# The last batch's side work in another order: smaller steps of the leftover choice, low parts of weights between VectorE and GpSimd

## The chip, the cores and the metric

One Trainium2 chip, one core. The metric is the device time of one execution in microseconds (us). The engines are TensorE (PE; PEld is its weight loading), VectorE (DVE), ScalarE (ACT), GpSimd (POOL) and SyncE (SP), whose queue issues most of the transfers.

## The reference

Attention over pooled keys and values (8 batches, 8 heads, 576 positions, head width 64), whose output, 4608 tokens of 512 numbers, goes through a mixture of 16 experts in 4 groups. Each token takes its best group and in it its best expert.

```python
scores = scale * np.matmul(q, k_p.transpose(0, 1, 3, 2))
...
g_idx = np.argmax(x @ w_group, axis=1)
...
e_idx = np.argmax(xg @ w_expert[g], axis=1)
...
h = np.maximum(xg[mask_e] @ w1[g, e], 0.0)
ye = h @ w2[g, e]
out[tok_idx] = combined[:, None] * ye
```

## The kernel before

**Batches and plans.** The work goes batch by batch. Strings of pieces (`START`, `FIRST`, `SECOND`, `STEADY`, `LAST`) write down by hand in which order the pieces are issued; each engine does its own instructions in just this order, and waits at each for what it needs. `LAST` is the plan of the last batch, in which there is no attention of a next batch to fill in.

**The main expert of a batch.** Almost all tokens of a batch choose one expert. Its weights are fetched and the whole batch goes through them. Every weight block is held as two fp32r parts: `m.cast:m:j` (ScalarE, line 579) makes the high part of quarter j of matrix m, `m.lo:m:j` (line 585) makes the low part by a subtraction, on GpSimd unless the piece ends in `:v` (VectorE). `m.up:f:h` is the first product for hidden block f and token half h: 12 matmuls (line 602) and a relu on ScalarE (line 604). `m.upd:f:h` makes the low part of the hidden values on VectorE (line 610 for the first half, the three instructions of line 615 for the second) and frees the accumulator. There are three of these (pool `ps_m`), so the fourth product after one waits for that one's `upd`. `m.down:z` is a piece of the second product, 8 matmuls (lines 631 and 642; 663 for the last 128 rows).

**Leftover tokens.** Tokens of other experts are collected in blocks of 32. `Left.place` counts and ranks them in steps, one for each `l.step` of the plan (lines 733 to 771, most on VectorE). `l.which` (lines 778 to 785, VectorE) then chooses the block's batch and expert, and SyncE loads the two numbers into registers (lines 786 to 788). Only then can `l.fetch_x` (line 834) fetch the two parts of that batch's x from memory into `pT` and `xr`, cleared by `l.xtiles` (line 824, GpSimd); `l.fetch_a` and `l.fetch_b` fetch the expert's weights behind it. `l.whole:c` (line 848) adds the two parts of x, for odd c on GpSimd, for even c on VectorE. `l.rows` (line 816) and `l.turn:c` (line 858) are TensorE pieces that stand in the plan between the last up products and the down products; `l.turn:3`, the first turn, reads what `l.whole:3` wrote. The rest of the block's products (lines 866 to 896) stands between later down pieces.

Of the kernel before, what the change touches and what calls it, by code (L numbers as in the profile page):

```python
# [30 lines left out]
BS = 32  # L31
# [34 lines left out]
x.su_:0 x.nm:0:p w.lo:1:1 m.down:10 m.down:11 m.down:12 w.cast:1:2 m.down:13 w.cast:1:3  # L66
"""
LAST = """
m.load:2:3 m.load:2:2 m.up:0:0 p.tail m.upd:0:0 m.lo:1:2:v m.up:0:1 l.step m.upd:0:1 m.up:1:0 l.step l.step m.upd:1:0 m.up:1:1 l.step l.step m.upd:1:1 l.xtiles
m.up:2:0 m.cast:2:1 l.step m.upd:2:0 l.step m.up:2:1 l.step m.upd:2:1 l.step m.up:3:0 l.step l.step m.upd:3:0 m.up:3:1 l.step l.step m.upd:3:1  # L70
m.up:5:0 l.step l.step l.step l.step m.upd:5:0 m.lo:1:3 m.cast:2:2 m.up:4:0 l.step l.step l.which m.lo:2:2:v m.upd:4:0 m.lo:2:1:v
m.up:6:0 m.cast:2:0 m.upd:6:0 m.up:5:1 m.lo:2:0:v m.up:4:1 m.up:6:1 m.cast:2:3 l.fetch_x l.tiles m.upd:5:1 m.upd:4:1 m.upd:6:1 l.slots m.down:0 m.down:1 l.fetch_a:1
m.up:7:0 l.fetch_b:1 m.upd:7:0 l.whole:4 l.whole:0 m.up:7:1 l.rows l.next_ l.whole:3 m.upd:7:1 l.turn:3 l.turn:4 m.down:12
l.whole:1 l.turn:1 l.turn:0 l.whole:2 m.lo:2:3:p m.down:2 m.down:3 l.turn:2 m.down:4 l.gather m.down:5 l.back m.down:6 l.up m.down:7 l.hback
m.down:8 l.down l.fetch_x l.fetch_a l.fetch_b m.down:13 m.down:9 m.down:10 l.slots m.down:11
# [4 lines left out]
def attn_moe(ctx: ExitStack, tc: tile.TileContext, q, k, v, wg, we, w1, w2, out):  # L80
    nc = tc.nc
# [603 lines left out]
    class Left:  # L685
# [22 lines left out]
        def place(s):  # L708

            kb = wk.tile([128, NC, 2, D], F32, name="kb").rearrange("p g x d -> p g (x d)")  # L710
            s.lt_, s.colf, tri = kb[:, 0], kb[:, 1], kb[:, 2]
            kp = wk.tile([128, 6, D], F32R, name="v6", bufs=2).rearrange("p g d -> p (g d)")
            onesr, trir = kp[:, 0:128], kp[:, 128:256]

            nc.gpsimd.affine_select(out=tri, in_=ones, pattern=[[1, 128]], compare_op=ALU.is_gt, fill=0.0, base=0, channel_multiplier=-1)
            nc.scalar.copy(out=trir, in_=tri)
            nc.scalar.copy(out=onesr, in_=ones)
            yield

            nc.gpsimd.iota(s.colf, [[0, 4], [1, BS]], base=0, channel_multiplier=0, allow_small_or_imprecise_dtypes=True)  # L720
            sl = sq.tile([128, NC * DM], F32, name="q")
            s.sl = [sl[:, 128 * c:128 * c + 128] for c in range(NC)]
            s.xg, s.xs, s.h = sl[:, 640:768], sl[:, 768:896], sl[:, 896:1152]
            s.hT = sl[:, 1152:1408].rearrange("p (t x) -> p t x", t=2)
            s.y = sl[:, 1408:1536]
            s.tmp = wk.tile([128, H * SP], F32, name="kT")
            kv = sk.tile([128, 5, 512], F32, name="kv").rearrange("p a x -> p (a x)")
            tot, rank = [kv[:, o:o + 640].rearrange("p (b c e) -> p b c e", b=B, c=NC) for o in (0, 640)]
            lf = loh.rearrange("p b c e -> p (b c e)")
            for lhs, dst in ((onesr, tot), (trir, rank)):  # L730
                for o, n in ((0, 320), (320, 320)):
                    ps = ps_t.tile([128, 512], F32, name="tp")
                    nc.tensor.matmul(ps[:, 0:n], lhsT=lhs, rhs=lf[:, o:o + n], start=True, stop=True)
                    nc.vector.tensor_copy(out=dst.rearrange("p b c e -> p (b c e)")[:, o:o + n], in_=ps[:, 0:n])
                    yield
            for c in range(1, NC):

                tt(out=rank[:, :, c, :], in0=rank[:, :, c, :], in1=tot[:, :, c - 1, :], op=ALU.add)
                tt(out=tot[:, :, c, :], in0=tot[:, :, c, :], in1=tot[:, :, c - 1, :], op=ALU.add)
                yield  # L740

            sc_ = sk.tile([128, 5, 512], F32, name="vv").rearrange("p a x -> p (a x)")
            nb, exc = sc_[:, 0:128], sc_[:, 128:256].rearrange("p (b e) -> p b e", e=NE)
            nbi = sc_[:, 256:384].bitcast(I32)
            ts(out=nb.rearrange("p (b e) -> p b e", e=NE), in0=tot[:, :, NC - 1, :], scalar1=float(BS - 1), scalar2=None, op0=ALU.add)
            nc.vector.tensor_copy(out=nbi, in_=nb)
            yield
            ts(out=nbi, in0=nbi, scalar1=5, scalar2=None, op0=ALU.logical_shift_right)
            nc.vector.tensor_copy(out=nb, in_=nbi)
            yield  # L750
            nc.vector.tensor_tensor_scan(out=s.cum, data0=ones, data1=nb, initial=0.0, op0=ALU.mult, op1=ALU.add)
            tt(out=exc.rearrange("p b e -> p (b e)"), in0=s.cum, in1=nb, op=ALU.subtract)
            yield

            for c in range(NC):
                stt(out=rank[:, :, c, :], in0=exc, scalar=float(BS), in1=rank[:, :, c, :], op0=ALU.mult, op1=ALU.add)
                yield
            stt(out=rank, in0=rank, scalar=1.0 + 2.0 ** 20, in1=loh.bitcast(F32), op0=ALU.add, op1=ALU.mult)
            red(out=s.pos, in_=rank, axis=AX.X, op=ALU.add)
            ts(out=s.pos, in0=s.pos, scalar1=-1.0 - 2.0 ** 20, scalar2=None, op0=ALU.add)  # L760
            yield

            for c, (o, n) in enumerate(CH):
                nc.gpsimd.iota(s.meta[:, c, :, 0], [[4 * S, B]], base=4 * (o - int(BIG)), channel_multiplier=4, allow_small_or_imprecise_dtypes=True)
                if c < 4:
                    nc.gpsimd.iota(s.meta[:, c, 0:1, 0], [[0, 1]], base=4 * (256 * (c // 2) + c % 2 - int(BIG)), channel_multiplier=8, allow_small_or_imprecise_dtypes=True)
            nc.gpsimd.tensor_copy(out=s.meta[:, :, :, 1], in_=gate.rearrange("p b c -> p c b"))
            nc.vector.memset(s.it, 0.0)

            ts(out=s.tmp[:, 0:1], in0=s.cum[:, B * NE - 1:B * NE], scalar1=-1.0, scalar2=0.0, op0=ALU.add, op1=ALU.max)  # L770
            nc.vector.tensor_copy(out=s.niti, in_=s.tmp[:, 0:1])
            yield
# [228 lines left out]
```

## Time and profile before

| what | us |
|---|---|
| median of 3 runs | 514.22 (513.57 to 514.29) |
| the profiled execution's own time | 514.15 |
| its span, first to last instruction | 512.4 |
| TensorE busy in it | 501.1 (98%) |
| VectorE busy | 345.6 (67%) |
| GpSimd busy | 281.6 (55%) |

Times in the profile count from the start of the span; the 1.75 us between the span and the execution's time lie outside it. A busy TensorE says only that matmuls are in flight. The mean granted TensorE clock is 0.993 of full speed. The last batch's up products begin at 447.77 us.

### The profile page before, as it was taken

The numbers are of one execution on the slowest core, as the hardware profiler recorded it, in microseconds if no ns is written. First come the engines' busy times: TensorE is split into PE (matmuls) and PEld (weight loads), VectorE is DVE, ScalarE is ACT, GpSimd is POOL, SyncE is SP. The second block draws the span as 40 slices with busy tenths as digits, with TensorE's granted clock in tenths as the row PEclk, the third lists the DMA queues.
The fourth block names the chain that finished last, engine by engine and source line by source line (L and its number), as shares of the span: only waits on it lengthen the run. The fifth ranks groups of instructions, "written<-read, shape, count | busy, mean of one in ns | idle before, by whom it ended". The sixth has DMA issues, their size and how long they took to land.

```text
span 512.4 us, 14902 instructions
## 1 busy us (share of the span) xinstructions
PE 501.1 (98%) x6085; PEld 440.1 (86%) x6085; DVE 345.6 (67%) x928; ACT 206.3 (40%) x385; POOL 281.6 (55%) x246
## 2 busy tenths in 40 slices
PE   8899999999999999999999999999999999998996
PEld 6688987998889978899789988899789988898976
DVE  6876877899385869486784768476784764199702
ACT  2354432545216542455216551455325551344212
POOL 2386666576518595476828585476947471830400
PEclk9799999999999999999999999999999999999999
DMA  8699299685428966954197615985055100923751
GB/s 279 191 260 205 24 280 236 124 192 137 77 92 242 265 106 176 318 150 80 29 308 213 151 26 138 368 311 89 1 191 192 43 3 22 304 96 114 271 172 58
DMA packets 118110, 83.70 MB, mean 163 GB/s; under 512 B 71034, under 2 KB 93818, under 8 KB 117784
## 3 DMA queue, kind: packets, MB, share of 16 engines
q1 hardware_dynamic: 113408, 75.67, 54.7%
q10 hardware_dynamic: 4600, 7.02, 4.0%
q8 instruction: 49, 0.80, 0.7%
q14 instruction: 21, 0.17, 0.1%
q0 software_dynamic: 32, 0.04, 0.0%
HBM read 77.28 MB, written 28.53 MB: 206 GB/s over the span
## 4 chain that ended last, share of the span: by engine, by line
PE 76%; DVE 10%; DMA 5%; ACT 2%; POOL 2%; issue 2%; SPq 1%; ACTq 0%; DVEq 0%; POOLq 0%
PE mm L602 30%; PE mm L631 27%; PE mm L642 4%; PE sc L396 4%; PE sc L336 4%; DMA vv<-in_v_dram 2%; DMA sw<-in_moe_w_dram 2%; PE tp L429 1%; PE mm L663 1%; POOL w L585 1%; DVE s L368 1%; DVE ht L615 1%; DVE pT L382 1%; PE tp L425 1%; DVE p L357 1%
## 5 line engine op out<-in xcount | busy, mean ns | idle before, releaser
L631 PE MATMUL mm<-w,ht 128*128 128x512 f32 x744 | 172.6, 385 | 0.0
L585 POOL TENSOR_TENSOR w<-sw,w 128x1024 fp32r<-128x1024 f32 (+2 forms) x86 | 145.2, 1711 | 33.7 <-ACT w L579 29.2
L631 PEld LDWEIGHTS mm<-w,ht 128*128 128x128 f32 x744 | 136.8, 189 | 25.2 <-issue 6.4
L602 PE MATMUL mm<-xb,w 128*128 128x288 f32 (+1 forms) x768 | 109.6, 294 | 1.7 <-DVE ht L610 1.7
L602 PEld LDWEIGHTS mm<-xb,w 128*128 128x128 f32 x768 | 100.7, 189 | 6.1 <-ACT w L579 2.2
L602 PE MATMUL mm<-xa,w 128*128 128x288 f32 (+1 forms) x768 | 100.2, 283 | 0.5 <-ACT xa L401 0.5
L602 PEld LDWEIGHTS mm<-xa,w 128*128 128x128 f32 x768 | 95.5, 190 | 2.2 <-ACT xa L401 0.9
L604 ACT ACTIVATE ht<-mm 128x288 fp32r<-128x288 f32 (+2 forms) x128 | 51.9, 410 | 87.1 <-PE mm L602 85.4
L375 POOL TENSOR_TENSOR p<-p,su 128x864 f32<-128x864 f32 (+2 forms) x30 | 40.3, 1343 | 78.6 <-DVE su L370 67.7
L579 ACT CAST w<-sw 128x1024 fp32r<-128x1024 f32 x64 | 66.7, 1042 | 31.5 <-DMA sw<-in_moe_w_dram 29.0
L615 DVE SCALAR_TENSOR_TENSOR ht<-mm,ht 128x64 fp32r<-128x64 f32 (+4 forms) x192 | 37.7, 252 | 25.8 <-ACT ht L604 25.5
L636 ACT ACTIVATE y<-mm,gm 128x512 f32<-128x512 f32 x31 | 21.2, 684 | 66.4 <-PE mm L631 66.4
L362 ACT ACTIVATE p<-p 128x864 f32<-128x864 f32 (+2 forms) x30 | 23.4, 780 | 37.5 <-DVE p L357 29.6
L368 DVE TENSOR_REDUCE s<-p 128x12 f32<-128x864 f32 (+2 forms) x30 | 25.8, 861 | 15.1 <-ACT p L362 15.1
L382 DVE STREAM_TRANSPOSE pT<-p 128x960 f32<-128x960 f32 (+2 forms) x30 | 29.2, 972 | 8.0 <-POOL p L375 7.2
L610 DVE SCALAR_TENSOR_TENSOR ht<-mm,ht 128x288 fp32r<-128x288 f32 (+1 forms) x64 | 26.9, 422 | 10.4 <-ACT ht L604 10.4
L642 PE MATMUL mm<-w,ht 128*128 128x512 f32 x128 | 29.5, 381 | 0.0
L336 PEld LDWEIGHTS sc<-kT,qT 64*32 64x32 f32 x2176 | 23.7, 105 | 6.3 <-issue 3.5
L336 PE MATMUL sc<-kT,qT 64*32 64x72 f32 x2176 | 28.5, 229 | 0.5 <-DVE qT L322 0.2
L675 DVE TENSOR_TENSOR y<-mm,y 64x512 f32<-64x512 f32 x8 | 5.5, 682 | 33.6 <-ACT y L647 20.2
L396 PE MATMUL sc<-pT,v 32*64 32x288 f32 (+2 forms) x384 | 26.9, 409 | 0.2 <-DVE p L357 0.2
L396 PE MATMUL tp<-pT,v 32*64 32x288 f32 (+2 forms) x384 | 26.9, 409 | 0.0
(227 smaller groups left out, 568.8 us busy)
## 6 DMA issues: line engine op xcount, KB each, us to landing
sw<-in_moe_w_dram SPq DMA_DIRECT2D x72, 512.0 KB
vv<-in_v_dram SPq DMA_DIRECT2D x27, 320.0 KB
q<-in_q_dram SPq DMA_DIRECT2D x112, 72.0 KB
kv<-in_k_dram SPq DMA_DIRECT2D x14, 512.0 KB
out_dram<-y ACTq DMA_DIRECT2D x23, 256.0 KB
xscr<-xa SPq DMA_DIRECT2D x5, 1152.0 KB
xscr<-xb SPq DMA_DIRECT2D x5, 1152.0 KB
xscr<-xb SPq DMA_DIRECT2D x3, 1280.0 KB
```

The source lines that it names most:

```text
L336: nc.tensor.matmul(ps[x][32 * g:32 * g + 32, SP * t:SP * t + SP], lhsT=s.qT[c][64 * x:64 * x + 64, g, 32 * t:32 * t + 32], rhs=s.kT[64 * x ...
L368: red(out=two[:, :, :, 0], in_=p.rearrange("p t (x s) -> p t x s", x=2), axis=AX.X, op=ALU.add)
L375: (nc.vector if eng == "v" else nc.gpsimd).tensor_tensor(out=p, in0=p, in1=bc(s.su[c][:, 0:w], SP), op=ALU.mult)
L382: nc.vector.transpose(out=s.pT[:, :, o:o + n].rearrange("p j (t i) -> p t j i", i=32), in_=probs[:, z:z + n // 32].rearrange("p t (j i) -> ...
L396: nc.tensor.matmul(banks[a][64 * x:64 * x + 64, 0:n], lhsT=s.v6[32 * a:32 * a + 32, 5 if x and i == 0 else j, :], rhs=s.pT[32 * a:32 * a + ...
L579: nc.scalar.copy(out=s.w[m, j][0], in_=raw)
L585: (nc.vector if eng == "v" else nc.gpsimd).tensor_tensor(out=wl[:, i:i + n], in0=s.raw[m, j][:, i:i + n], in1=wh[:, i:i + n].bitcast(F32), ...
L602: nc.tensor.matmul(ps[:, 0:n], lhsT=l[:, kc, fs], rhs=apart(s.a.xt[hf][:, r, kc]), start=(kc == 0 and i == 0), stop=(kc == 3 and i == 2))
L604: nc.scalar.activation(out=halves(ht[:, sl]), in_=joined(ps[:, 0:n]), func=AF.Relu)
L615: stt(out=ht[:, at:at + hi - lo], in0=ps[:, a, lo:hi], scalar=0.0, in1=ht[:, t + lo:t + hi].bitcast(F32), op0=ALU.max, op1=ALU.subtract)
L631: nc.tensor.matmul(ps, lhsT=s.ht[f][:, 640 * l + o:640 * l + o + 128], rhs=apart(s.w[2, f // 2][r][:, f % 2, :]), start=(i == 0), stop=(i ...
L642: nc.tensor.matmul(ps, lhsT=s.ht[f][:, 512:640], rhs=apart(s.w[2, f // 2][r][:, f % 2, :]), start=(i == 0), stop=(i == 15))
```

## The change

Two things change, both of them for the last batch. In `Left.place` the first step is cut in two: the triangle mask and the column numbers (GpSimd) come first, the two fp32r casts (ScalarE) in a step of their own. And `LAST` is written anew in its first lines: the first step stands ahead of everything, the other steps are shared out differently among the up products, the low parts 1:2, 1:3 and 2:0 go to GpSimd ahead of the clearing of `pT` and `xr`, and 2:1 and 2:2 stay on VectorE, the first right behind `m.upd:2:0`, the second right behind `m.upd:5:1`. The order of the up products is the same. From `MANUAL` on, every line number is one lower.

```diff
 LAST = """
-m.load:2:3 m.load:2:2 m.up:0:0 p.tail m.upd:0:0 m.lo:1:2:v m.up:0:1 l.step m.upd:0:1 m.up:1:0 l.step l.step m.upd:1:0 m.up:1:1 l.step l.step m.upd:1:1 l.xtiles
-m.up:2:0 m.cast:2:1 l.step m.upd:2:0 l.step m.up:2:1 l.step m.upd:2:1 l.step m.up:3:0 l.step l.step m.upd:3:0 m.up:3:1 l.step l.step m.upd:3:1
-m.up:5:0 l.step l.step l.step l.step m.upd:5:0 m.lo:1:3 m.cast:2:2 m.up:4:0 l.step l.step l.which m.lo:2:2:v m.upd:4:0 m.lo:2:1:v
-m.up:6:0 m.cast:2:0 m.upd:6:0 m.up:5:1 m.lo:2:0:v m.up:4:1 m.up:6:1 m.cast:2:3 l.fetch_x l.tiles m.upd:5:1 m.upd:4:1 m.upd:6:1 l.slots m.down:0 m.down:1 l.fetch_a:1
+l.step m.load:2:3 m.load:2:2 m.lo:1:2 m.lo:1:3 m.up:0:0 p.tail m.upd:0:0 m.up:0:1 l.step m.cast:2:0 m.upd:0:1 m.lo:2:0 m.up:1:0 l.step l.step m.upd:1:0 m.up:1:1 l.step l.step m.upd:1:1 l.xtiles
+m.up:2:0 m.cast:2:1 l.step m.upd:2:0 m.lo:2:1:v m.up:2:1 l.step m.upd:2:1 m.up:3:0 l.step l.step m.upd:3:0 m.up:3:1 l.step l.step m.cast:2:2 m.upd:3:1
+m.up:5:0 l.step l.step m.upd:5:0 m.up:4:0 l.step l.step l.step l.step m.upd:4:0 m.up:6:0 l.step m.upd:6:0 m.up:5:1 l.step l.which m.upd:5:1 m.up:4:1 m.lo:2:2:v m.upd:4:1 m.up:6:1 m.cast:2:3 l.fetch_x l.tiles m.upd:6:1 l.slots m.down:0 m.down:1 l.fetch_a:1
 m.up:7:0 l.fetch_b:1 m.upd:7:0 l.whole:4 l.whole:0 m.up:7:1 l.rows l.next_ l.whole:3 m.upd:7:1 l.turn:3 l.turn:4 m.down:12
...
             nc.gpsimd.affine_select(out=tri, in_=ones, pattern=[[1, 128]], compare_op=ALU.is_gt, fill=0.0, base=0, channel_multiplier=-1)
+            nc.gpsimd.iota(s.colf, [[0, 4], [1, BS]], base=0, channel_multiplier=0, allow_small_or_imprecise_dtypes=True)
+            yield
             nc.scalar.copy(out=trir, in_=tri)
             nc.scalar.copy(out=onesr, in_=ones)
             yield
-
-            nc.gpsimd.iota(s.colf, [[0, 4], [1, BS]], base=0, channel_multiplier=0, allow_small_or_imprecise_dtypes=True)
```

On VectorE before, from the `upd` of the up product 2:0 (line 610) on, only steps of the ranking follow until the `upd` of 2:1 (line 615):

```order
L610 SCALAR_TENSOR_TENSOR ht<-mm,ht 128x288
L738 TENSOR_TENSOR kv<-kv 128x8x16
L739 TENSOR_TENSOR kv<-kv 128x8x16
L738 TENSOR_TENSOR kv<-kv 128x8x16
L739 TENSOR_TENSOR kv<-kv 128x8x16
L615 SCALAR_TENSOR_TENSOR ht<-mm,ht 128x144
```

The same place in the changed kernel:

```order
L609 SCALAR_TENSOR_TENSOR ht<-mm,ht 128x288
L584 TENSOR_TENSOR w<-sw,w 128x1024
L737 TENSOR_TENSOR kv<-kv 128x8x16
L738 TENSOR_TENSOR kv<-kv 128x8x16
L614 SCALAR_TENSOR_TENSOR ht<-mm,ht 128x144
```

The low part 2:1 (line 585, now 584) has come in here, and one step has moved behind the `upd` of 2:1.

On VectorE before, this stands between the last ranks and the first instruction of `l.which` (line 778), with the `upd` of 5:0 as the only one of line 610:

```order
L756 SCALAR_TENSOR_TENSOR kv<-vv,kv 128x8x16 x4
L610 SCALAR_TENSOR_TENSOR ht<-mm,ht 128x288
L758 SCALAR_TENSOR_TENSOR kv<-kv,loh 128x640
L759 TENSOR_REDUCE pos<-kv 128x40
L760 TENSOR_SCALAR pos<-pos 128x40
L768 MEMSET it 128x1
L770 TENSOR_SCALAR kT<-cum 128x1
L771 CAST niti<-kT 128x1
L778 TENSOR_SCALAR kb<-cum,it 128x128
```

The same place in the changed kernel, with the `upd`s of 5:0, 4:0 and 6:0:

```order
L609 SCALAR_TENSOR_TENSOR ht<-mm,ht 128x288
L755 SCALAR_TENSOR_TENSOR kv<-vv,kv 128x8x16 x4
L609 SCALAR_TENSOR_TENSOR ht<-mm,ht 128x288
L757 SCALAR_TENSOR_TENSOR kv<-kv,loh 128x640
L758 TENSOR_REDUCE pos<-kv 128x40
L759 TENSOR_SCALAR pos<-pos 128x40
L609 SCALAR_TENSOR_TENSOR ht<-mm,ht 128x288
L767 MEMSET it 128x1
L769 TENSOR_SCALAR kT<-cum 128x1
L770 CAST niti<-kT 128x1
L777 TENSOR_SCALAR kb<-cum,it 128x128
```

The `upd`s of 4:0 and 6:0, which stood behind `l.which`, now stand ahead of it.

On GpSimd before, in the last batch (line 585 twice for 1:0 and 1:1, then the mask, the column numbers, the two clearings, 1:3, and the first number of `meta`):

```order
L585 TENSOR_TENSOR w<-sw,w 128x1024 x2
L715 AFFINE_SELECT kb<-ones 128x128
L720 IOTA kb 128x128
L824 MEMSET pT 128x2304
L824 MEMSET xr 128x2304
L585 TENSOR_TENSOR w<-sw,w 128x1024
L764 IOTA meta 128x8
```

The same place in the changed kernel:

```order
L584 TENSOR_TENSOR w<-sw,w 128x1024 x2
L714 AFFINE_SELECT kb<-ones 128x128
L715 IOTA kb 128x128
L584 TENSOR_TENSOR w<-sw,w 128x1024 x3
L823 MEMSET pT 128x2304
L823 MEMSET xr 128x2304
L763 IOTA meta 128x8
```

Three low parts (1:2, 1:3, 2:0) now stand ahead of the clearings, where one stood behind them. The orders of TensorE and of SyncE are the same in both kernels.

## Rows read from the trace of the kernel before

**Rows 1.** The page's busy lines and the shares of the chain that ended last.

```profile
PE 501.1 (98%) x6085; PEld 440.1 (86%) x6085; DVE 345.6 (67%) x928; ACT 206.3 (40%) x385; POOL 281.6 (55%) x246
...
PE 76%; DVE 10%; DMA 5%; ACT 2%; POOL 2%; issue 2%; SPq 1%; ACTq 0%; DVEq 0%; POOLq 0%
```

**Rows 2.** Waits, 444 to 513 us: who waited for whom, us, times, longest.

```profile
POOL pT L848 <- DMA xr<-xscr: 23.8, 1, 23.8
...
PE mm L602 <- DVE ht L610: 1.7, 1, 1.7
```

**Rows 3.** TensorE's timeline: start, us, line, tiles, count, [idle before <-releaser].

```profile
464.53 1.63 PE L602 MATMUL mm<-xb,w 128*128 128x288 f32 x12
467.84 3.24 PE L602 MATMUL mm<-xb,w 128*128 128x288 f32 x24 [1.68 <-DVE ht L610]
...
477.53 1.26 PE L816 MATMUL tp<-kT,q 128*128 128x2 f32 x10
478.79 1.09 PE L858 MATMUL tp<-ident,pT 128*128 128x128 f32 x8
...
502.61 5.52 PE L663 MATMUL mm<-w,ht 128*128 128x256 f32 x48
```

**Rows 4.** VectorE's timeline in the last batch.

```profile
450.34 2.69 DVE L585 TENSOR_TENSOR w<-sw,w 128x1024 fp32r<-128x1024 f32 x1
...
456.35 0.46 DVE L610 SCALAR_TENSOR_TENSOR ht<-mm,ht 128x288 fp32r<-128x288 f32 x1
456.72 0.28 DVE L738 TENSOR_TENSOR kv<-kv 128x128 f32<-128x128 f32 x1
...
464.50 0.19 DVE L760 TENSOR_SCALAR pos<-pos 128x40 f32<-128x40 f32 x1
...
466.14 0.14 DVE L785 TENSOR_SCALAR ki<-ki 128x1 int32<-128x1 int32 x1
466.20 1.22 DVE L585 TENSOR_TENSOR w<-sw,w 128x1024 fp32r<-128x1024 f32 x1
467.33 0.45 DVE L610 SCALAR_TENSOR_TENSOR ht<-mm,ht 128x288 fp32r<-128x288 f32 x1
467.70 1.22 DVE L585 TENSOR_TENSOR w<-sw,w 128x1024 fp32r<-128x1024 f32 x1
```

**Rows 5.** ScalarE's timeline: casts of weights (1:2, 1:3 and 2:1).

```profile
445.69 1.05 ACT L579 CAST w<-sw 128x1024 fp32r<-128x1024 f32 x1 [0.49 <-ACT y L636]
...
448.45 1.04 ACT L579 CAST w<-sw 128x1024 fp32r<-128x1024 f32 x1
...
456.21 1.04 ACT L579 CAST w<-sw 128x1024 fp32r<-128x1024 f32 x1
```

**Rows 6.** SyncE's timeline: the issue of the first fetch of x.

```profile
468.66 0.36 SPq L834 DMA_DIRECT2D pT<-xscr  x1
```

**Rows 7.** GpSimd's timeline: a clearing, a low part, and `l.whole:3` alone.

```profile
444.69 2.01 POOL L824 MEMSET pT<- 128x2304 f32 x1
...
449.58 2.36 POOL L585 TENSOR_TENSOR w<-sw,w 128x1024 fp32r<-128x1024 f32 x1 [0.92 <-ACT w L579]
...
477.23 1.50 POOL L848 TENSOR_TENSOR pT<-pT,xr 128x512 f32<-128x512 f32 x1 [23.83 <-DMA xr<-xscr]
```

**Rows 8.** VectorE's timeline at the program's start.

```profile
2.68 1.11 DVE L113 TENSOR_SCALAR hm<-flath 128x40 f32<-128x40 f32 x1
```

**Rows 9.** GpSimd's timeline at the program's start.

```profile
2.57 1.18 POOL L117 MEMSET p<- 128x1280 f32 x1
```

**Rows 10.** Stretches: us; busy PE, PEld, DVE, ACT, POOL; granted clock; DMA share, GB/s.

```profile
16.00:20.00 4.00, 3.16 (x37) 2.65 (x36) 3.34 (x14) 0.99 (x3) 0.10 (x1) 0.72 0.23 45
20.00:24.00 4.00, 3.38 (x72) 2.80 (x73) 3.19 (x7) 2.37 (x5) 2.79 (x5) 0.50 1.00 323
24.00:28.00 4.00, 3.52 (x57) 2.29 (x55) 1.25 (x4) 2.06 (x5) 4.00 (x6) 0.93 1.09 297
...
466.00:470.00 4.00, 2.32 (x19) 2.16 (x18) 3.97 (x8) 0.87 (x3) 0.00 (x0) 1.00 0.19 32
```

## Prediction

> **What bounds the kernel now.** I read the page's busy lines and chain first: TensorE is busy 98% of the span and holds 76% of the chain [rows 1]. So a change of order can win only where TensorE stands idle, and lose wherever it makes TensorE wait. The waits of the last batch come next: TensorE waits once there, 1.7 us, for an instruction of line 610 on VectorE [rows 2]. TensorE's timeline shows where: 5:1 begins at 464.53, then TensorE is idle 1.68 us, and 4:1 begins at 467.84 [rows 3]. It waits for the accumulator of 4:0, freed by the `upd` at 467.33, which stands on VectorE behind the whole choice of the leftover block (done with line 785 at 466.28) and behind a low part of 1.13 us, the distance from 466.20 to 467.33 [rows 4]. This stall is the one thing to be won here: 1.68 us, 0.33%.
>
> There is a second place, and no wait is listed for it, since it only just holds. `l.turn:3` starts on TensorE at 478.79, right after the ten small products of `l.rows` [rows 3]. It needs `l.whole:3`, which GpSimd runs from 477.23 for 1.50 us, to 478.73, after waiting for the transfer of x [rows 7, 2]. Result and reader are 0.06 us apart: TensorE would have arrived at 477.11 without its stall, and would then have waited here for the same 1.68 us. So the stall at 466 costs nothing by itself; **the chain that decides is choice on VectorE, registers on SyncE, transfer of x, `l.whole:3`, first turn**. Its lengths: line 785 ends at 466.28, the first fetch issues at 468.66, 2.38 us later [rows 4, 6]; the sum of both parts begins at 477.23, 8.57 us after the issue; its first use is 1.56 us after that. From the first turn to the last matmul's end, 508.13, TensorE's timeline has no idle time [rows 3]. So the end moves one for one with the end of `l.whole:3`, whatever happens ahead of it, unless TensorE itself is later.
>
> **The change, part by part.**
>
> *The choice on VectorE.* VectorE meets the `upd` of 2:0 at 456.35 in both orders, since that waits for its relu; what VectorE saves before this (the low part 1:2, 2.69 us) only turns into waiting. From 456.35 to 466.28 it is full. The new order puts three more instructions into this stretch and takes none out: the low part 2:1, and the `upd`s of 4:0 and 6:0. The low part takes 1.13 us (the 2.69 of the first one lay beside a low part on GpSimd, below), an `upd` of line 610 takes 0.37 (467.33 to 467.70) [rows 4]. Before the low part can start, its cast must end: ScalarE casts 2:1 from 456.21 to 457.25, behind the relu of 2:0 as before [rows 5], and VectorE, free at 456.72, waits 0.53 us. Sum: 0.53 + 1.13 + 0.37 + 0.37 = **2.40 us later**, so the choice ends at 468.7 where it ended at 466.3. Fewer gaps between dependent steps may give back 0.2.
>
> *The fetch.* SyncE's order is the same, with the same loads behind the fetch, so I keep 2.38 and 8.57 us: issue at 471.1, x there at 479.6, `l.whole:3` done at 481.1. The clearings on GpSimd, which the fetch must follow, end by about 459.2 in the new order (three low parts of 2.36 us, the last from about 452.9, then two clearings of 2.0 [rows 7]), 12 us before it: covered.
>
> *The stall at 466.* It goes. The `upd` of 4:0 comes ahead of line 758. That of 6:0 follows line 760, which ended at 464.69 and now ends 0.53 + 1.13 + 0.37 = 2.03 later: 466.7 to 467.1, while 6:1 can't start before 467.6 (4:1 at 466.16, and about half of the 3.24 us that two products take [rows 3]). The `upd` of 5:1 now stands behind the choice, at 468.7 to 469.2, and may hold the first down piece 0.1 to 0.2 us. TensorE then reaches the first turn at about 477.1 and **waits there about 4 us**, until 481.2.
>
> *The low parts on GpSimd.* 1:2 and 1:3 need their casts, which end at 446.7 and 449.5 [rows 5], so both are there by 451.9, and 5:0 needs 1:2 at about 460. The low part 2:0 is due at the first down piece, 469. All covered by up products; without that cover each would cost its 2.36 us. The high part of 2:0 moves ahead of the relu of 1:0 on ScalarE and delays it by less than its own 1.04 us [rows 5]; VectorE has its copies of line 734 to do till then. Cutting the first step in two moves two casts and changes no due time.
>
> *The shared work of VectorE and GpSimd.* A low part on VectorE beside one on GpSimd took 2.69 us and not 1.22, until GpSimd's ended at 451.94 [rows 4, 7]. In the new order GpSimd's low parts lie beside instructions that read the accumulators. But the two clearings (455.2 to 459.2) now lie beside two additions of the ranking and the low part 2:1. Whether a clearing holds such an instruction up no row shows for sure. The nearest: at the start a scaling of 128x40 took 1.11 us and ended with a clearing of 1.18 us beside it [rows 8, 9]. If additions were held like this, one step's pair would pass at the end of the first and of the second clearing, and the low part would end at about 461.05 in place of 458.4: 2.65 us more in the chain. Lower bound 0, upper 2.65; I take 0, because the held instruction of the start has one input and the additions two, a different kind. The Trainium skill, SBUF — State Buffer, section Who interferes with whom, says that an instruction of VectorE with two inputs in SBUF contends with one of GpSimd that reads SBUF, and not with one that only writes it. By that rule the term is 0 and by the row read straight it is 2.65; the 2.69 us beside a reading GpSimd agrees with the rule, and no row here has an addition beside a clearing.
>
> *TensorE's clock.* The stretch from 16 to 24 us has the granted clock at 0.72 and then 0.50, that is at 1.2 GHz, after few and small matmuls and waits; from 24 to 28 it is back at 0.93. In these 12 us it gave away (0.28 + 0.50 + 0.07) x 4 = 3.4 us of full-speed time. The 1.68 us of idling at 466 left it at 1.00 [rows 10]. The new wait of 4 us follows ten products of two columns that take 1.26 us, so TensorE does next to nothing for over 5 us, three times what left the clock alone. Bounds 0 and 3.4 us; half of a low stretch would pass while TensorE waits anyway, so I take **1.7**. The Trainium skill, TensorE: Matmul & The Clock Gate, Part 1, says "the default state is throttled, and activity releases the throttle"; the 0.50 of 20 to 24 us agrees.
>
> **Sum.** Against the profiled execution's 514.15 us: 514.15 + 2.4 + 1.7 = 518.25. The median of the three runs is 514.22, so about **518.3**.
>
> **The rivals.**
> 1. *The fetch is late, the clock stays.* For it: the stall of 1.68 us did not move it. Against: 5 us are much more. 514.15 + 2.4 = 516.6 us.
> 2. *The clearings hold VectorE as well.* For it rows 8 and 9; against it that they show another kind of instruction. The chain is 2.4 + 2.65 = 5.05 late: 519.2 with a full clock, 520.9 with 1.7 of the clock.
> 3. *Faster: the transfer of x is not bound to its issue.* If the transfer's 8.57 us shrink by more than 2.4, because the weight loads behind it compete with it less, `l.whole:3` ends no later than before and the stall's 1.68 us become a gain: with a transfer under 4.5 us the full 514.15 - 1.68 = 512.5; at 6.2 us it breaks even. For it: other loads run in the same stretch. Against: SyncE issues the same loads in the same order behind it.
> 4. *No difference.* VectorE's chain is shorter than I add up, or the cast of 2:1 comes earlier, and the choice ends within 0.5 us of its old time. It would need the three instructions to fit in gaps, and there are none between 456.35 and 466.28. 514 us.
>
> **How the numbers follow.** Late fetch with a fallen clock 50%, 517.5 to 519.8 us; rival 1 24%; rival 2 12%; rival 3 6%; rival 4 8%. The likeliest gives 518.3. The range 516.0 to 520.8 takes in the first two and over half of the third, and leaves out some 18%. A measurement of this kernel can tell about 0.2% (1 us) from no change: faster 0.06, the same 0.09, slower 0.85.
>
> **What would show it.** In the new profile TensorE's wait at 466 is gone and one of about 4 us stands ahead of the first turn, ended by GpSimd's `l.whole:3`; line 784 (the last of the choice) ends at 468.7; the fetch of x issues at 471.1 and lands 8.5 us later; the low part 2:1 on VectorE takes 1.2 us (a hold by the clearings would show as 2 us or more there or on lines 737 and 738); the granted clock dips to half for some us near 482. I am wrong if the sum of the two parts of x starts by 478: then the chain was not what I took it for. I am wrong in size if the clock stays, or if the clearings hold VectorE.

## The result and the profile after

The changed kernel takes 519.42 us (median of 4 runs, 518.59 to 519.75) against 513.89 (513.11 to 514.29, 4 runs) for the one before: ratio 1.0101, 95% interval 1.0081 to 1.012. It is slower by 1%. The profiled execution took 518.59 us, its span is 516.9 us, and its last batch begins at 447.52 us, 0.25 us earlier than before. Line numbers are one lower than in the rows of before.

The page's busy lines and the chain that ended last, after:

```profile
PE 503.2 (97%) x6085; PEld 441.3 (85%) x6085; DVE 342.7 (66%) x926; ACT 206.3 (40%) x385; POOL 286.5 (55%) x248
...
PE 78%; DVE 10%; DMA 5%; POOL 2%; ACT 2%; issue 2%; SPq 1%; ACTq 0%; DVEq 0%; POOLq 0%
```

TensorE has the same 6085 matmuls as in [rows 1] and is busy 2.1 us longer. A matmul that is the same and lasts longer points at the clock. The waits of the last batch, 444 to 518 us (who waited for whom: us, times, longest):

```profile
POOL pT L847 <- DMA xr<-xscr: 18.6, 1, 18.6
...
PE tp L857 <- POOL pT L847: 4.1, 1, 4.1
```

The 1.7 us for VectorE of [rows 2] are gone. In their place TensorE waits 4.1 us for GpSimd's sum of x. TensorE's timeline (start, us, count, idle before and its releaser):

```profile
464.29 4.57 PE L601 MATMUL mm<-xb,w 128*128 128x288 f32 x36
...
475.30 1.26 PE L815 MATMUL tp<-kT,q 128*128 128x2 f32 x10
480.64 1.97 PE L857 MATMUL tp<-ident,pT 128*128 128x128 f32 x8 [4.09 <-POOL pT L847]
...
507.15 5.52 PE L662 MATMUL mm<-w,ht 128*128 128x256 f32 x48
```

The up products now run through 466 without a gap, where [rows 3] have 1.68 us of idle time. The ten small products come 2.23 us earlier than there (475.30 against 477.53), the first turn 1.85 us later (480.64 against 478.79). The same eight turn products took 1.09 us before and take 1.97 now. From the first turn to the end of the last matmul it is 507.15 + 5.52 - 480.64 = 32.03 us, where [rows 3] give 29.34. The two differences, 1.85 and 2.69, make the 4.5 us by which the span has grown. VectorE, where the time of the first turn is made:

```profile
456.11 0.46 DVE L609 SCALAR_TENSOR_TENSOR ht<-mm,ht 128x288 fp32r<-128x288 f32 x1 [0.28 <-ACT ht L603]
457.04 1.23 DVE L584 TENSOR_TENSOR w<-sw,w 128x1024 fp32r<-128x1024 f32 x1 [0.48 <-ACT w L578]
458.19 0.29 DVE L737 TENSOR_TENSOR kv<-kv 128x128 f32<-128x128 f32 x1
...
468.05 0.14 DVE L784 TENSOR_SCALAR ki<-ki 128x1 int32<-128x1 int32 x1
468.11 0.57 DVE L614 SCALAR_TENSOR_TENSOR ht<-mm,ht 128x144 fp32r<-128x144 f32 x3
```

The low part 2:1 is the second row; the choice ends at 468.19, where [rows 4] have 466.28. Behind it SyncE's first fetch of x, and on GpSimd the last early low part, the two clearings and `l.whole`:

```profile
470.63 0.36 SPq L833 DMA_DIRECT2D pT<-xscr  x1
```

```profile
452.69 2.38 POOL L584 TENSOR_TENSOR w<-sw,w 128x1024 fp32r<-128x1024 f32 x1 [0.99 <-ACT w L578]
455.00 2.02 POOL L823 MEMSET pT<- 128x2304 f32 x1
456.96 2.02 POOL L823 MEMSET xr<- 128x2304 f32 x1
...
479.09 3.17 POOL L847 TENSOR_TENSOR pT<-pT,xr 128x512 f32<-128x512 f32 x2 [18.63 <-DMA xr<-xscr]
```

The fetch issues 2.44 us behind the choice, x is there 8.46 us later, the first turn starts another 1.55 us later: 2.38, 8.57 and 1.56 in [rows 6, 7]. Stretches of the end (us; busy PE, PEld, DVE, ACT, POOL; granted clock; DMA share; GB/s):

```profile
475.30:479.32 4.02, 1.26 (x12) 1.15 (x10) 0.28 (x1) 0.41 (x1) 0.23 (x1) 1.00 0.99 395
479.32:486.15 6.83, 5.51 (x18) 4.53 (x19) 6.41 (x18) 0.58 (x1) 5.25 (x3) 0.50 0.57 177
486.15:490.00 3.85, 3.85 (x23) 3.48 (x22) 1.29 (x2) 1.28 (x2) 0.00 (x0) 1.00 1.00 322
```

TensorE works 1.26 of the first 4 us, and then the clock stands at 0.50 (1.2 GHz) for 6.83 us, of which 5.51 lie behind the start of the turn. Half of 5.51 is 2.75, next to the 2.69 us that the tail has grown by.

### The profile page after: what moved, and what is told of

It reads as the page before. It is cut to its first block, busy times and chain, and to the rows that moved or that the text cites. A ratio compares the mean times of both kernels' runs of the same rounds, so it can differ in the third digit from the quotient of the medians.

```text
span 516.9 us, 14905 instructions
## 1 busy us (share of the span) xinstructions
PE 503.2 (97%) x6085; PEld 441.3 (85%) x6085; DVE 342.7 (66%) x926; ACT 206.3 (40%) x385; POOL 286.5 (55%) x248
## 4 chain that ended last, share of the span: by engine, by line
PE 78%; DVE 10%; DMA 5%; POOL 2%; ACT 2%; issue 2%; SPq 1%; ACTq 0%; DVEq 0%; POOLq 0%
PE mm L630 29%; PE mm L601 28%; PE mm L641 4%; PE sc L395 4%; PE sc L335 4%; DMA vv<-in_v_dram 1%; DMA xr<-xscr 1%; PE tp L428 1%; DMA sw<-in_moe_w_dram 1%; PE mm L662 1%; POOL w L584 1%; PE tp L424 1%; DVE ht L614 1%; DVE s L367 1%; DVE ht L609 1%
## 5 line engine op out<-in xcount | busy, mean ns | idle before, releaser
L584 POOL TENSOR_TENSOR w<-sw,w 128x1024 fp32r<-128x1024 f32 (+2 forms) x88 | 150.0, 1729 | 36.8 <-ACT w L578 36.6
L630 PEld LDWEIGHTS mm<-w,ht 128*128 128x128 f32 x744 | 136.8, 189 | 25.2 <-issue 6.4
L641 PEld LDWEIGHTS mm<-w,ht 128*128 128x128 f32 x128 | 25.0, 198 | 3.9 <-issue 0.2
```

Of the source, the lines that this page charges most:

```text
L584: (nc.vector if eng == "v" else nc.gpsimd).tensor_tensor(out=wl[:, i:i + n], in0=s.raw[m, j][:, i:i + n], in1=wh[:, i:i + n].bitcast(F32), ...
L630: nc.tensor.matmul(ps, lhsT=s.ht[f][:, 640 * l + o:640 * l + o + 128], rhs=apart(s.w[2, f // 2][r][:, f % 2, :]), start=(i == 0), stop=(i ...
L641: nc.tensor.matmul(ps, lhsT=s.ht[f][:, 512:640], rhs=apart(s.w[2, f // 2][r][:, f % 2, :]), start=(i == 0), stop=(i == 15))
```

## The experiments

The table gathers what each profiled execution shows. Choice, x and turn: the end of the choice (line 784; 785 before) and the start of the first turn, both counted from the first up product of the last batch, and the time from the issue of the fetch to the start of `l.whole`. Near-idle: the ten small products (1.26 us) and the wait behind them. In experiment 12 the dummies stand between the two, so its 2.4 us are 1.26 and 1.12 us apart from each other. Low: what of the stretch with the clock at 0.50 lies behind the start of the turn. Tail: from the first turn to the end of the last matmul. Ratio: to the kernel before on the same chip, with its 95% interval. The columns up to tail are of one execution each and leave out where its last batch begins, which lies anywhere from 445.91 (experiment 2) to 448.88 us (experiment 4); the median is over all executions.

| kernel | choice | x | turn | near-idle | low | tail | median us | ratio |
|---|---|---|---|---|---|---|---|---|
| before | 18.52 | 8.57 | 31.02 | 1.3 | 0 | 29.34 | 513.89 | 1 |
| changed | 20.67 | 8.46 | 33.12 | 5.3 | 5.51 | 32.03 | 519.42 | 1.0101 (1.0081 to 1.012) |
| 1 choice first | 19.33 | 8.87 | 32.20 | 3.0 | 0 | 29.34 | 515.92 | 1.0036 (1.0018 to 1.0053) |
| 2 low part 2:1 late | 20.16 | 8.68 | 32.84 | 4.4 | 3.41 | 31.02 | 518.45 | 1.0078 (1.0054 to 1.0101) |
| 3 dummies ahead | 20.65 | 9.90 | 34.54 | 2.9 | 2.82 | 30.70 | 517.95 | 1.0069 (1.0043 to 1.0094) |
| 4 low part 1:2 back | 20.65 | 8.55 | 33.19 | 5.4 | 3.75 | 31.16 | 519.03 | 1.0082 (1.0058 to 1.0105) |
| 5 other order of loads | 20.64 | 8.65 | 33.28 | 5.5 | 4.85 | 31.70 | 518.82 | 1.009 (1.0064 to 1.0116) |
| 6 early choice | 16.99 | 8.92 | 29.90 | 2.3 | 0 | 29.34 | 513.65 | 0.9988 (0.9966 to 1.0011) |
| 7 early, other order | 17.00 | 8.81 | 29.80 | 2.2 | 0 | 29.35 | 513.47 | 0.9992 (0.9974 to 1.001) |
| 9 before, other order | 18.51 | 8.63 | 31.06 | 1.3 | 0 | 29.35 | 514.04 | 0.9992 (0.9973 to 1.0011) |
| 10 x alone | 20.66 | 8.42 | 33.08 | 5.3 | 4.72 | 31.64 | 518.36 | 1.0087 (1.0071 to 1.0102) |
| 11 early, x alone | 17.00 | 8.76 | 29.74 | 2.2 | 0 | 29.35 | 513.03 | 0.9983 (0.9966 to 1.0) |
| 12 dummies behind | 20.66 | 9.58 | 34.23 | 2.4 | 0 | 29.69 | 517.5 | 1.009 (1.006 to 1.0119) |
| 13 early, x cut | 17.01 | 5.49 | 28.75 | 1.3 | 0 | 31.15 | 513.39 | 0.9991 (0.9976 to 1.0006) |

**Experiments 1 and 2: what the three added instructions cost.** In the edits of plans below only the changed part of each long line stands. The first keeps the new order of the steps and the low parts on GpSimd, and puts the low part 2:1 and the `upd`s of 4:0 and 6:0 behind the choice; the second moves the low part alone.

```diff
 experiment 1
-m.upd:2:0 m.lo:2:1:v m.up:2:1
+m.upd:2:0 m.up:2:1
...
-m.upd:4:0 m.up:6:0 l.step m.upd:6:0 m.up:5:1 l.step l.which m.upd:5:1
+m.up:6:0 l.step m.up:5:1 l.step l.which m.upd:4:0 m.upd:6:0 m.lo:2:1:v m.upd:5:1
 experiment 2
-m.upd:2:0 m.lo:2:1:v m.up:2:1
+m.upd:2:0 m.up:2:1
...
-l.which m.upd:5:1
+l.which m.lo:2:1:v m.upd:5:1
```

> The changed kernel, but the low part 2:1 and the updates of 4:0 and 6:0 stand behind the choice on VectorE; the three low parts stay on GpSimd. My theory (the end follows the chain choice, fetch of x, sum, first turn): the choice ends within 0.3 us of its time in the kernel before (466.3), the fetch issues at 468.6, the first turn starts at 478.7, TensorE waits about 0.7 us at 466 and 0.9 us ahead of the turn, the clock stays at 1.00, and the time is that of the kernel before within 0.2%. Rival A (the rearranged GpSimd queue costs): it stays 4 to 5 us slower. Rival B (the stall at 466 is what the kernel before loses): about 1 us faster than before, ratio 0.998.

> The changed kernel, but only the low part 2:1 moves behind the choice on VectorE; the updates of 4:0 and 6:0 stay ahead of it. My theory: the choice ends 1.6 us earlier than in the changed kernel, about 466.6, the fetch issues at 469.0, TensorE waits 2.4 us ahead of the first turn, which starts at 479.0; without a fall of the clock the profiled time is 514.2 to 514.7, with one some 1 to 2.5 us more. Rival A (GpSimd's queue): 518 to 519 as the changed kernel. This one also tells how long a wait it takes for the clock to fall.

Against the changed kernel, taking the low part out brings the choice forward by 20.67 - 20.16 = 0.51 us (1.6 expected), and taking the two `upd`s out as well by another 0.83. The choice is then still 0.81 us behind that of before (at most 0.3 expected). VectorE's timeline of experiment 1 shows why the low part is worth so little:

```profile
456.62 0.46 DVE L609 SCALAR_TENSOR_TENSOR ht<-mm,ht 128x288 fp32r<-128x288 f32 x1 [0.28 <-ACT ht L603]
457.00 0.28 DVE L737 TENSOR_TENSOR kv<-kv 128x128 f32<-128x128 f32 x1
457.20 0.28 DVE L738 TENSOR_TENSOR kv<-kv 128x128 f32<-128x128 f32 x1
458.09 0.59 DVE L614 SCALAR_TENSOR_TENSOR ht<-mm,ht 128x144 fp32r<-128x144 f32 x3 [0.61 <-ACT ht L603]
```

Between the `upd` of 2:0 and that of 2:1 only one step is left, where before there are two. Without the low part VectorE waits there 0.61 us for the relu of 2:1. The low part and the wait for its cast, 0.48 + 1.13 us, fill that wait and put what follows 1.00 us later. Half a us of this is made good further on, over half of it at the `upd` of 4:0, whose relu VectorE waits for in experiment 2 and not in the changed kernel. The `upd`s of 2:1 and of 4:0, in experiment 2:

```profile
455.97 0.59 DVE L614 SCALAR_TENSOR_TENSOR ht<-mm,ht 128x144 fp32r<-128x144 f32 x3 [0.61 <-ACT ht L603]
...
461.85 0.46 DVE L609 SCALAR_TENSOR_TENSOR ht<-mm,ht 128x288 fp32r<-128x288 f32 x1 [0.20 <-ACT ht L603]
```

and in the changed kernel:

```profile
458.59 0.58 DVE L614 SCALAR_TENSOR_TENSOR ht<-mm,ht 128x144 fp32r<-128x144 f32 x3
...
463.96 0.45 DVE L609 SCALAR_TENSOR_TENSOR ht<-mm,ht 128x288 fp32r<-128x288 f32 x1
```

Counted from the first up product (445.91 and 447.52), experiment 2 is 1.01 us ahead of the changed kernel at the first of the two and 0.50 at the second. In experiment 1, the step that has moved behind the `upd` of 2:1 takes 0.52 us of the 0.81 there (the steps of before start at 456.72 and 457.24); the other 0.3 us lie in small gaps, and I did not trace them to one place. Experiment 1 still has a stall of 1.36 us ahead of 4:1, as in the kernel before, and TensorE waits another 1.74 us at the first turn: that wait is set by x, not by the stall. Its clock stayed at 1.00 and its tail is that of before, to the hundredth; its time is 0.36% over that of before, where at most 0.2% was expected. In experiment 2, the clock fell in the profiled execution, at 479.31, 0.56 us after the first turn had begun.

**Experiments 3 and 12: the clock.** Nine dummy products (18 passes in the trace) give TensorE work in its wait: ahead of the ten small products in experiment 3, behind them in 12.

```diff
 experiment 3
-m.up:7:1 l.rows l.next_ l.whole:3 m.upd:7:1 l.turn:3
+m.up:7:1 l.fill:9 l.rows l.next_ l.whole:3 m.upd:7:1 l.turn:3
 experiment 12
-m.up:7:1 l.rows l.next_ l.whole:3 m.upd:7:1 l.turn:3
+m.up:7:1 l.rows l.next_ l.whole:3 m.upd:7:1 l.fill:9 l.turn:3
 both
+        def fill(s, z):
+            ps = ps_t.tile([128, 512], F32, name="tp")
+            for i in range(z):
+                nc.tensor.matmul(ps[:, 0:256], lhsT=ones, rhs=ones.unsqueeze(1).broadcast_to([128, 2, 128]), start=True, stop=True)
```

> The changed kernel, with nine products of ones by ones (128x256, some 0.43 us each, their result not read) put on TensorE between the last up product and the ten small products ahead of the first turn. My theory: the wait of 4.1 us is nearly filled, the first turn still starts at 480.6, the clock stays at 1.00, and the time falls by the clock's share alone, about 2.7 us: 515.9 profiled, ratio to the kernel before 1.004. Rival C (the clock's dip costs nothing, the late end has another cause): 518 to 519 as the changed kernel, or more for the added products.

> The changed kernel with nine dummy products (18 passes, some 4 us) between the ten small products and the first turn, where TensorE otherwise waits 4.1 us; earlier the same nine stood ahead of the ten small ones and left 2.9 us of near-idling, and the clock still fell. They write a buffer that nobody reads. Theory (TensorE's near-idling of over 5 us lowers the clock, and that costs half of the low stretch that lies behind the start of the turn): only the ten small products and at most 0.5 us of idling are left, the clock stays at 1.00, the turn starts when it did or up to 0.3 us later, from the turn to the last product 29.4 us and not 32.0: about 516.3. Rival (the clock's fall has another cause): a low stretch all the same near 480, 518.6 to 519.4.

In experiment 3 (517.95 us, 515.9 expected) the clock fell all the same, at 480.81, in the 2.9 us of small products and waiting that were left. In experiment 12 (517.5 us, 516.3 expected) it stayed. Its stretches ahead of and behind the turn:

```profile
475.50:481.90 6.40, 5.33 (x30) 4.49 (x28) 1.54 (x2) 0.41 (x1) 1.50 (x2) 1.00 1.02 378
481.90:488.00 6.10, 5.87 (x35) 5.13 (x36) 5.89 (x19) 1.41 (x3) 4.01 (x3) 1.00 0.30 90
```

Here TensorE works 5.33 of the 6.4 us ahead of the turn and is granted 1.00 on both sides of it; the tail is 29.69 us, 2.34 less than in the changed kernel, and 0.18 of it is a wait of the second turn for an accumulator that the small products still held. So the clock's 2.7 us come from TensorE's near-idling. The time did not show it fully: x landed 9.6 us after its issue in this execution, 1.1 us later than in the changed kernel, which leaves 1.2 of the 2.34 us, and the ratio's interval overlaps that of the changed kernel. One of the six executions took 522.1 us, the other five 517.3 to 518.1; the ratio takes in all six. Why x is slow in both kernels with dummies (9.90 and 9.58, against 8.4 to 8.9 where x is fetched whole without them) was not tried.

**Experiment 4: the low parts on GpSimd.** The low part 1:2 goes back to VectorE, ahead of everything that counts.

```diff
-m.lo:1:2 m.lo:1:3 m.up:0:0 p.tail m.upd:0:0 m.up:0:1
+m.lo:1:3 m.up:0:0 p.tail m.upd:0:0 m.lo:1:2:v m.up:0:1
```

> The changed kernel, with the low part 1:2 back on VectorE where it stood before (right behind the update of 0:0), so that GpSimd makes one low part fewer. My theory: VectorE only waits less ahead of 456 us, the choice ends at the same time within 0.2 us, and the time is that of the changed kernel within 1 us (518.0 to 519.6). Rival D (VectorE as a whole is the bound, and each low part taken from it counts): 1 to 2.7 us slower than the changed kernel. Rival A (GpSimd's queue): some 1 to 2 us faster.

The choice ends 20.65 us after the first up product as in the changed kernel (20.67), and the time is the same within its interval. Which engine makes this low part is worth nothing here.

**Experiments 5, 9, 10 and 11: is x late because of the weights beside it?** In 5 and 9 the fourth quarter of the weights is fetched first. In 10 all weight loads are held back until x is there; 11 does that with the early choice of experiment 6.

```diff
 experiments 5, 7 and 9
-            for j in range(4):
+            for j in (3, 0, 1, 2) if first else range(4):
 experiments 10 and 11
         def fetch_a(s, first=None):
+            if first:
+                nc.gpsimd.memset(s.wa[0][0:1, 0, 0:1], 0.0)
...
-m.down:1 l.fetch_a:1
-m.up:7:0 l.fetch_b:1 m.upd:7:0
+m.down:1
+m.up:7:0 m.upd:7:0
...
-l.rows l.next_ l.whole:3
+l.rows l.whole:3 l.fetch_a:1 l.fetch_b:1 l.next_
```

> The changed kernel with one difference: the fourth quarter of the leftover block's first weights is fetched first. Its buffer comes free only after the fourth low part, at about 484, so on SyncE's queue all four quarters now go out behind the transfer of x instead of three of them beside it. Theory of the prediction (the first turn starts at choice + registers + transfer + 1.55 us): the choice stays at 20.7 us after the first up product; x alone is 1.2 MB of the 2.7 MB that moved together in 8.5 us, so the transfer takes 5.5 to 6.5 us; TensorE's wait ahead of the first turn falls from 4.1 to 1.5 to 2.1; with the clock left alone about 514, with a low stretch of some us about 515.5. Rival (the transfer's length is a latency that other loads do not change): 8.5 us, wait 4.1, 519.4 as the changed kernel. Second rival (the weights now come too late for their first use at 497.7): a new wait on TensorE after 495.

> The kernel before with the weights behind x alone. Theory (in the kernel before the stall at 466 and the wait for x end 0.06 us apart, so that neither alone is worth anything): x comes 2 to 3 us earlier, TensorE's stall of 1.68 us stays, TensorE arrives at the first turn when it did, 514.1, ratio 1.000. Rival (x alone set the end in the kernel before): faster by up to 1.7 us, 512.5.

Both tell nothing on x: three loads still went out beside it, and the fourth to be issued waited, though another quarter came fourth. SyncE in experiment 5 (its four loads span 13.19 us, in the changed kernel 13.0):

```profile
472.71 13.19 SPq L837 DMA_DIRECT2D sw<-in_moe_w_dram  x4
```

I read this as the quarters getting their buffers in the order of their fetches and not by their numbers, so that the edit only renamed them. What they do show is how well a kernel repeats: 518.82 beside 519.42, 514.04 beside 514.09.

> The changed kernel with all eight loads of the leftover block's weights held back until x is there: a clearing of one element of their first buffer stands on GpSimd behind the third l.whole, and the loads stand behind it on SyncE's queue. (The order of the four quarters alone, tried before, did not hold them back: three of them still went out beside x.) Theory (the transfer is long because x shares the DMA engines with three weight loads: 1.2 of 2.7 MB): x takes 5 to 6.5 us after its issue and not 8.5, the wait ahead of the first turn falls from 4.1 to 1.1 to 2.1 us, and the time to about 514 with the clock left alone, 515 to 516 with a low stretch. Rival (the 8.5 us are the length of this fetch by itself): x at 8 us or more, wait about 4, 518.5 to 519.4. Against the edit itself: the weights come some 7 us later, at about 490, ahead of their first use at 497.7; a new wait on TensorE after 495 would show that they don't.

In experiment 10 SyncE's loads do come behind x, and x is no faster. The transfers of 470 to 480 us in it (GB/s in 40 slices of 0.25 us, and the issues):

```profile
GB/s 0 0 0 33 0 0 479 37 147 111 221 221 406 332 406 442 553 295 479 442 406 332 516 479 332 442 442 553 258 516 332 221 102 0 0 0 0 0 0 0
...
pT<-xscr SPq DMA_DIRECT2D x1, 1152.0 KB
xr<-xscr SPq DMA_DIRECT2D x1, 1152.0 KB
```

x alone is two transfers of 1152 KB, 2.36 MB, twice what the expectation of experiment 5 took for it. It moves from 471.5 to 478.2, from 473 on at some 420 GB/s (the mean of the slices up to 477.75). The Trainium skill, DMA: Bandwidth & Descriptors, section Specifications, gives 435 GB/s as the ceiling of the fabric; the slices agree, as a mean. So x, once under way, goes near that ceiling, and the weights behind it cost it nothing (8.42 us without them, 8.46 with them). Rival 3's transfer of 4.5 us was not to be had: 2.36 MB at 420 GB/s are 5.6 us without the start.

> The early choice and x alone on the DMA engines. The early choice left 1.07 us of waiting ahead of the first turn (choice 17.0 us after the first up product, transfer 8.9). If x alone is 2 us or more faster, that wait goes: TensorE reaches the first turn at 28.8 us after the first up product and goes on at once, the span is 510.2 where the early choice has 511.3, about 512.5 us, ratio 0.997. If the transfer is not shorter alone: as the early choice, 513.6.

The same with the early choice: 8.76 us, a wait of 0.92 us left ahead of the turn, and its time (513.03 against 513.65) is no shorter than that of experiment 6 by more than the runs scatter.

**Experiments 6 and 7: the choice made earlier.** The steps are packed closer and the low parts 2:0, 2:1 and 2:2 follow the choice on VectorE; 7 adds the other order of loads, which does nothing, so it is 6 over again.

```diff
-l.step m.load:2:3 m.load:2:2 m.lo:1:2 m.lo:1:3 m.up:0:0 p.tail m.upd:0:0 m.up:0:1 l.step m.cast:2:0 m.upd:0:1 m.lo:2:0 m.up:1:0 l.step l.step m.upd:1:0 m.up:1:1 l.step l.step m.upd:1:1 l.xtiles
+l.step l.step m.load:2:3 m.load:2:2 m.lo:1:2 m.lo:1:3 m.up:0:0 p.tail m.upd:0:0 m.up:0:1 l.step l.step m.upd:0:1 m.up:1:0 l.step l.step m.upd:1:0 l.xtiles m.up:1:1 l.step l.step m.upd:1:1
-m.up:2:0 m.cast:2:1 l.step m.upd:2:0 m.lo:2:1:v m.up:2:1 l.step m.upd:2:1 m.up:3:0 l.step l.step m.upd:3:0
+m.up:2:0 m.cast:2:1 l.step l.step l.step l.step m.upd:2:0 m.up:2:1 l.step l.step m.upd:2:1 m.up:3:0 l.step l.step l.step l.step m.upd:3:0 m.cast:2:0
...
-m.up:5:0 l.step l.step m.upd:5:0 m.up:4:0 l.step l.step l.step l.step m.upd:4:0 m.up:6:0 l.step m.upd:6:0 m.up:5:1 l.step l.which m.upd:5:1
+m.up:5:0 m.upd:5:0 m.up:4:0 m.up:6:0 l.step l.which m.upd:4:0 m.lo:2:1:v m.upd:6:0 m.up:5:1 m.lo:2:0:v m.upd:5:1
```

> The changed kernel with its steps of the choice packed closer and earlier among the up products, and the low parts 2:0, 2:1 and 2:2 on VectorE behind the choice (1:2 and 1:3 stay on GpSimd); the upd of 4:0 behind the choice's last line, but in time. Theory: the choice ends 16.7 us after the first up product instead of 20.7 (18.5 before), the transfer takes 8.5 us, the first turn could start at 29.1 us after it; TensorE, without the stall at 466, gets there at 29.0 us, so it waits neither at 466 nor at the turn, and the 1.68 us of the stall become a gain: 512.4, ratio 0.9967 to before. Rival (the chain is not the choice but something that stays, such as the clearings or the loads): turn at 31 us or later as before, 514 or more. Rival 2 (the choice can't be moved up, because VectorE waits for the relus): choice at 18 us or later, a wait of over 1 us ahead of the turn, 514 to 516.

> Both of the two before: the early choice, and the weights behind x. If the early choice alone already lets TensorE arrive last, x being 2 to 3 us earlier still is worth nothing more: 512.4, the same as the early choice alone. If the early choice alone leaves a wait ahead of the first turn, this one takes it away: 512.4 all the same. If neither holds and the time stays at 514 or more, TensorE is held by something else.

TensorE in experiment 6:

```profile
464.59 4.57 PE L601 MATMUL mm<-xb,w 128*128 128x288 f32 x36
...
475.39 1.26 PE L815 MATMUL tp<-kT,q 128*128 128x2 f32 x10
477.73 1.09 PE L857 MATMUL tp<-ident,pT 128*128 128x128 f32 x8 [1.07 <-POOL pT L847]
```

The choice ends at 16.99 us (16.7 expected), the stall at 466 is gone and the clock stays. A wait of 1.07 us ahead of the turn is left, which was not expected: x took 8.92 us and not 8.5. The turn starts 1.12 us sooner than before, counted from the first up product, and the tail is that of before: the 1.12 us are in the trace. In the time they are not proven: 513.65 us in experiment 6, where 512.4 was expected, and ratios of 0.9988, 0.9992 and 0.9983 in experiments 6, 7 and 11, all on the side of faster, no interval clear of 1.

**Experiment 13: fewer bytes ahead of the first turn.** Since x is as long as its bytes, the columns that the first two turns read are fetched first, on top of experiment 6.

```diff
-            for i in range(2):
-                nc.sync.dma_start(out=s.xh[i], in_=xscr[bass.ds(s.rb, 1)].rearrange("o p i g s -> p (o i) g s")[:, i], cond=s.some)
+            for o, n in ((384, S - 384), (0, 384)):
+                for i in range(2):
+                    nc.sync.dma_start(out=s.xh[i][:, :, o:o + n], in_=xscr[bass.ds(s.rb, 1)].rearrange("o p i g s -> p (o i) g s")[:, i, :, o:o + n], cond=s.some)
```

> The early choice, with the fetch of x cut by columns: the 192 columns of the first two turns come first, in both parts, then the other 384. The runs with x alone showed that the transfer's 8.4 to 8.9 us are not shared with the weights: x is 2 x 1152 KB, 2.36 MB, which at the 437 GB/s seen there takes 5.4 us by itself. Theory (the transfer is as long as its bytes): the first third is 0.79 MB, 1.8 us at that rate, so it lands 3.6 us earlier, at about 5.2 us after the issue; l.whole:3 is done some 2.5 us before TensorE gets to the first turn, the wait of 1.07 us that the early choice left is gone, span 510.2 and about 512.5 us, 0.3% under before. Rival (the smaller pieces, 768 and 1536 bytes in a row and not 9216, cost the engines more than the cut saves, or the first additions wait for all four transfers): x no sooner than 8.5 us, a wait of 1 us or more, 513.6 or slower.

The first third came 5.49 us after its issue, as expected, and TensorE starts the first turn without a wait, 28.75 us after the first up product. But the gain is given back. The waits that stand behind it in that execution:

```profile
PE tp L858 <- POOL pT L848: 0.7, 1, 0.7
PE mm L630 <- POOL w L584: 0.6, 1, 0.6
```

The other columns came at 478.70, 11.0 us after the first issue where the uncut x takes 8.9, and with them `l.whole`, the next turns and GpSimd's last low part came late; the tail is 31.15 us instead of 29.34, and the two waits are 1.3 of these 1.8 us. The median is 513.39 us, where 512.5 was expected. No version tried beats the kernel before by more than its measurement can tell.

## Why the prediction was right, point by point

**The chain.** It held in 13 of the 14 executions of the table: choice, 2.4 us of registers, the transfer, 1.55 us of `l.whole:3`, first turn; these parts add up to the start of the turn. In experiment 13, where x came early, TensorE itself arrived last. The stall at 466 was worth nothing by itself, as experiment 1 shows with both waits in one execution.

**The choice, 2.40 us.** Measured 2.15 (20.67 against 18.52). That the sum came out near is luck, since its terms did not. The wait for the cast (0.48, forecast 0.53) and the low part (457.04 to 458.19, forecast 1.13) are there as priced, yet they cost only 0.51 us more than the order without them, since VectorE would have waited for relus instead. The two `upd`s cost 0.83 (forecast 0.74). Of the other 0.81 us, 0.52 is the step that moved behind the `upd` of 2:1 and the rest lies in small gaps; the prediction did not price either. The sentence that failed is "the new order puts three more instructions into this stretch and takes none out": it counted instructions and took VectorE to be full in the new order too, where it is full only in the old one.

**The fetch.** 2.38 and 8.57 us were kept; 2.44 and 8.46 came. Issue 470.63 (forecast 471.1), wait ahead of the turn 4.09 us (about 4).

**Clearings and low parts.** The low part lay from 457.04 to 458.27 beside the clearing of `xr` (456.96 to 458.98) and took 1.23 us, as without one (1.22 in [rows 4]); an addition of the ranking beside the same clearing, at 458.19, took 0.29 (0.28 in [rows 4]). So the term is 0 and rival 2 is out. These are the rows that were missing: two inputs in SBUF beside a GpSimd that only writes. By the rule of the Trainium skill, SBUF — State Buffer, section Who interferes with whom, such an instruction does not contend; the trace agrees. The low parts on GpSimd are covered: TensorE's only wait of the last batch is that at the first turn, and experiment 4 shows that 1:2 is worth nothing on the other engine.

**The clock, 1.7 us.** The mechanism was right, the size was not: 2.69 us in the profiled execution. The step that missed is "half of a low stretch would pass while TensorE waits anyway". The low stretch was 6.83 us, worth 3.4 us of full-speed time, just the upper bound that the start of the program gave. But the clock fell only when TensorE had waited 2.76 of its 4.09 us, so 1.32 us of the stretch lay in the wait, a fifth of it and not half. In the six executions in which it fell, the tail grew by half the low time behind the turn, to within 0.1 us: from 2.82 us and 1.36 in experiment 3 to 5.51 and 2.69 in the changed kernel. Where in the wait the clock falls differs from one execution to the next. Experiment 4, with the same order on TensorE and a wait of 4.16 us, has it fall 2.35 us after the start of the ten small products (at 478.99, for 6.83 us, the turn starting at 482.07), where the changed kernel has 4.02:

```profile
475.00:479.00 4.00, 2.90 (x25) 2.80 (x23) 0.46 (x1) 0.82 (x2) 0.00 (x0) 1.00 1.00 422
479.00:483.00 4.00, 0.93 (x5) 0.90 (x6) 2.53 (x7) 0.00 (x0) 2.48 (x2) 0.50 1.04 355
483.00:487.00 4.00, 4.00 (x18) 3.38 (x17) 3.79 (x12) 0.58 (x1) 3.00 (x2) 0.65 0.24 77
```

There 3.08 us of the stretch lay in the wait, nearly the half that was forecast, and the tail grew by 1.82 us. So the forecast share can be met; the changed kernel's profile and experiments 4, 5 and 10, all with this wait, paid 1.82 to 2.69 us.

**The sum.** The choice was 0.25 us shorter than forecast, the batch began 0.25 sooner, the fetch was 0.05 shorter and the clock cost 1.0 more: 518.25 becomes 518.7, and the profiled execution took 518.59. The median of the runs, 519.42, lies 0.8 us above that execution, which was the shortest of the four.

## What to carry to other kernels

Before filling a stall, find the next wait behind it: where two waits end within 0.06 us of each other, ending one is worth nothing, and what is done to end it can lengthen the other. An instruction put into an in-order queue costs its length less the waits that it fills, so count the waits of the new order and not only its instructions. And a wait of TensorE that follows small products is dearer than its own length: price the lower clock behind it too.

## What was not expected of the hardware

- Near-idling of 2.9 us lowered the clock in one execution (experiment 3) and of 3.0 us did not in another (experiment 1). Both are single executions, and what decided it is open.
- The mean granted clock of an execution does not tell whether it paid this price. In experiment 2 the profiled execution has the highest mean but one of eight (0.996; six have 0.986 or 0.99) and the shortest time (515.78 us; those six 518.18 to 519.17), and yet its clock stood at 0.50 from 479.31 to 482.72. The mean counts the whole program, and this execution lacks the low stretch at the start that [rows 10] show; its last batch begins 1.6 us earlier than in the changed kernel. What the other seven paid is not in a trace. The granted clock in 40 slices of the span, in tenths, of the kernel before and of experiment 2:

```profile
PEclk9799999999999999999999999999999999999999
PEclk9999999999999999999999999999999999999899
```

- The transfer of x was not lengthened by the 1.5 MB of weights issued behind it on the same queue: 8.42 us alone, 8.46 with them.
- Cutting it into pieces of 768 and 1536 bytes in a row brought the first third 3.4 us forward and the rest 2.1 us back.
